# One explicit list of steps for an attention-and-mixing kernel on one core

**The chip, the cores and the metric.** The kernel runs on one core of a Trainium2 chip. The metric is the device time of one execution in microseconds (us). A "span" is the time from the first to the last instruction in a profile; the measured time is 1 to 2 us longer (192.06 against 190.2 in the profiled run of before). Runs are called fast or slow by their time and granted TensorE clock; only fast runs are compared here, and the times and ranges given leave slow ones out.

## The reference, cut to what matters

Four batches, 8 heads, 768 positions, head size 64. Windowed attention with four sink positions makes x; a mixing block follows.

```python
scores = (q @ k.T) / sqrt(64)              # kept: the 4 sinks, and 128 positions back
x      = softmax(scores) @ v               # laid out as (batch, 768, 512)

theta  = x @ w_theta
y      = w_tok_r @ (x * cos(theta)) + w_tok_i @ (x * sin(theta))    # over the 768 positions
u      = x + y
out    = u + max(u @ w_ch, 0)
```

The kernel works on 16 head pairs (four for each batch) and 23 blocks of 128 output rows, plus a last one in halves. Its words, which the argument uses: *scores* (q, k on TensorE, three groups to a pair), *values* (E times v), *theta* (8 matmuls of 512 columns for each of three groups of a batch), *mixing* (12 such matmuls to a block), *channel* (4 to a block). Before scores q and k must be cast to bf16 and transposed; before theta x must be transposed, before channel u.

## The kernel before

The program fixes each engine's order itself: every call puts its instructions at the end of its engines' queues in the order of the source, and semaphores do the rest. It is written as loops over pairs and blocks. This is the loop of the second half:

```python
    for b in range(2, B):
        p = b - 1                                  # batch p is mixed while batch b has its attention
        for hp in range(HP):
            i = b * HP + hp
            blk = (p, hp)
            ...
            scores(i, 0)                           # matmuls AND the exponential that frees their bank
            scores(i, 1)
            ...
            mix(*blk, 0, 8)                        # eight matmuls in one piece
            ...
            scores(i, 2)
            mix(*blk, 8, 12)                       # the other four
            masks(i, 0, 2)
            done(*blk)                             # add(), then dma_u(): the transpose of u
            if hp > 0:
                values(i - 1, 0)
                values(i - 1, 1)
                norm(i - 1)
                dma_x(b, hp - 1)                   # the transpose of one slice of x
            ...
        i = b * HP + HP - 1
        values(i, 0)
        values(i, 1)
        norm(i)
        dma_x(b, HP - 1)                           # the last slice of x ...
        mix(p, 4, 0, 12)
        done(p, 4)
        ...
        theta(b, 0)                                # ... and its first reader
```

Nearly all transposes of u, and those of x from batch 1 on (its last slice excepted), are DMA transposes that SyncE issues, in one queue with all loads and stores:

```python
    def dma_u(b, t):
        nc.sync.dma_start_transpose(out=uT_of(b, t), in_=u_t[b, t].rearrange("p c n -> p (c n)"))

    def done(b, t):
        add(b, t)
        dma_u(b, t)
        waiting.append((b, t))                     # its channel product comes two blocks later
```

The softmax here doesn't subtract the row's maximum and nothing guards it: scores larger than these inputs give would overflow.

## Time and profile before

| | before |
|---|---|
| time, median of 3 runs | 192.33 us (192.32 to 192.81) |
| span of the profiled run | 190.2 us |
| busy: TensorE, VectorE, ScalarE, GpSimd | 169.5, 112.2, 98.2, 73.2 us |
| read from memory | 25.82 MB |
| DMA transposes | 38: 23 of u, 11 of x, 4 of q and k |

The prediction shows the busy shares, the slices, the stretches and the gap at 110 us. One more view belongs beside them. It lists what TensorE's instructions waited for: engine, bank and line of the waiting instruction, the releaser, then us in total, number of waits and the longest.

```profile
PE sc L345 <- DMA xT<-x_nat: 4.0, 2, 2.8
PE sm L345 <- DVE qkT L118: 1.5, 1, 1.5
PE sc L252 <- DMA qkT<-qk: 1.4, 1, 1.4
```

The largest of them are waits of theta (line 345) on a transposed x and on a bank, and of scores (252) on transposed keys.

### The profile page before, as it was taken

To read this page: it belongs to the slowest core of one execution; us is meant where nothing else is said; L and a number is where in the kernel's file an instruction comes from. 1 tells how busy PE (TensorE), PEld (TensorE's weight loads), DVE (VectorE), ACT (ScalarE), POOL (GpSimd) and SP (SyncE) were. 2 spreads that over 40 slices of the span, in tenths; PEclk is the share of its full clock that TensorE was granted. 3 is DMA by queue.
4 is the path that set the end of the run, shared out by engine and by line. 5 is a ranking of instruction groups with operands and counts; after the bars stand their busy time and mean duration, and the time that the engine had idled before them with its cause. 6 is when DMAs were issued, how large, how long until landed. Compare 5 with 4: busy or idle time off the path is not lost.

```text
span 190.2 us, 3823 instructions
## 1 busy us (share of the span) xinstructions
PE 169.5 (89%) x1505; PEld 88.8 (47%) x1505; DVE 112.2 (59%) x193; ACT 98.2 (52%) x129; POOL 73.2 (38%) x95
## 2 busy tenths in 40 slices
PE   7899889599999999698999837999799899999971
PEld 2345465255565565353665413443455444444541
DVE  7556874848656562776777620476757626624442
ACT  3775495977673923699658104497348135300000
POOL 7675556988953737528114610306400000000000
PEclk9999999999999999999999997999999999999997
DMA  5999999999999999999999999379946550514343
GB/s 164 243 332 219 304 394 324 317 337 339 173 357 258 190 295 208 214 306 259 214 156 221 197 177 201 63 133 281 200 96 126 124 127 7 188 30 108 86 138 110
DMA packets 81154, 39.06 MB, mean 205 GB/s; under 512 B 68208, under 2 KB 75632, under 8 KB 81136
## 3 DMA queue, kind: packets, MB, share of 16 engines
q1 hardware_dynamic: 78832, 38.74, 88.6%
q0 software_dynamic: 2304, 0.07, 1.1%
q8 instruction: 12, 0.20, 0.4%
q14 instruction: 6, 0.05, 0.1%
HBM read 25.82 MB, written 6.29 MB: 169 GB/s over the span
## 4 chain that ended last, share of the span: by engine, by line
PE 65%; DMA 12%; DVE 9%; ACT 7%; SPq 3%; issue 2%; POOL 1%; ACTq 0%; POOLq 0%
PE mm L393 21%; PE sc L393 7%; PE mm L421 6%; PE sc L252 6%; PE sc L345 6%; DMA qkT<-qk 5%; PE sm L297 3%; PE sm L225 3%; DMA kf<-in_k_dram 2%; DMA uT<-u 2%; PE sm L378 2%; ACT E L264 2%; DVE x_nat L310 2%; PE sm L443 2%; PE av L297 2%
## 5 line engine op out<-in xcount | busy, mean ns | idle before, releaser
L264 ACT ACTIVATE E<-sc 128x1024 bf16<-128x1024 f32 x48 | 47.3, 1029 | 18.1 <-PE sc L252 12.7
L393 PE MATMUL mm<-zz,wrT 128*128 128x512 bf16 x108 | 41.9, 388 | 0.0
L393 PE MATMUL mm<-zz,wiT 128*128 128x512 bf16 x108 | 41.7, 386 | 0.0
L272 DVE TENSOR_TENSOR E<-E,mask 128x768 bf16<-128x768 bf16 (+1 forms) x28 | 27.3, 974 | 9.2 <-ACT E L264 9.2
L367 DVE TENSOR_TENSOR zz<-cs,x_nat 128x1024 bf16<-128x1024 bf16 x24 | 17.2, 757 | 14.2 <-ACT cs L358 14.1
L421 PE MATMUL mm<-wch,uT 128*128 128x512 bf16 x92 | 23.1, 379 | 0.7 <-DMA uT<-u 0.7
L399 DVE TENSOR_TENSOR u<-mm,x_nat 128x512 bf16<-128x512 f32 x18 | 12.4, 691 | 15.5 <-PE mm L393 15.4
L393 PEld LDWEIGHTS <-wrT 128*128 128x128 bf16 x138 | 13.6, 98 | 16.4 <-issue 2.4
L345 PE MATMUL sc<-wth,xT 128*128 128x512 bf16 x64 | 16.3, 388 | 4.8 <-DMA xT<-x_nat 4.0
L357 ACT ACTIVATE cs<-sc,half_pi 128x1024 bf16<-128x1024 f32 x7 | 7.8, 1117 | 24.6 <-PE sc L345 24.6
L252 PE MATMUL sc<-qkT 64*128 64x256 bf16 x192 | 17.9, 281 | 2.8 <-DMA qkT<-qk 1.4
L393 PEld LDWEIGHTS <-wiT 128*128 128x128 bf16 x138 | 13.7, 99 | 13.8 <-issue 0.8
L297 PEld LDWEIGHTS <-E 128*128 128x128 bf16 x480 | 16.6, 97 | 6.0 <-DVE E L272 1.7
L423 DVE SCALAR_TENSOR_TENSOR of<-mm,u 128x512 f32<-128x512 f32 x23 | 15.8, 689 | 5.1 <-PE mm L421 5.1
L345 PEld LDWEIGHTS <-xT 128*128 128x128 bf16 x96 | 9.2, 99 | 19.9 <-DMA xT<-x_nat 5.3
L114 POOL TENSOR_SCALAR qk<-two 128x768 bf16<-128x768 f32 x8 | 7.5, 951 | 23.5 <-DMA two<-in_k_dram 11.4
L114 POOL TENSOR_SCALAR qk<-qf 128x768 bf16<-128x768 f32 x10 | 10.3, 1028 | 14.1 <-PE sm L225 6.3
L114 POOL TENSOR_SCALAR vx<-vf 128x768 bf16<-128x768 f32 x12 | 12.1, 1011 | 8.5 <-DMA vf<-in_v_dram 7.5
L114 POOL TENSOR_SCALAR qk<-kf 128x768 bf16<-128x768 f32 x10 | 13.6, 1356 | 1.0 <-DMA kf<-in_k_dram 0.6
L252 PEld LDWEIGHTS <-qkT 64*128 64x128 bf16 x192 | 6.9, 96 | 14.6 <-issue 8.8
L421 PEld LDWEIGHTS <-uT 128*128 128x128 bf16 x92 | 8.6, 98 | 10.0 <-DMA uT<-u 1.6
L118 DVE COPY qkT<-sm 128x384 f32<-128x384 f32 (+1 forms) x14 | 7.6, 555 | 7.1 <-PE sm L225 4.1
(103 smaller groups left out, 234.3 us busy)
## 6 DMA issues: line engine op xcount, KB each, us to landing
out_dram<-of SPq DMA_DIRECT2D x23, 256.0 KB, 2.6
vf<-in_v_dram SPq DMA_DIRECT2D x12, 384.0 KB, 7.3
qf<-in_q_dram SPq DMA_DIRECT2D x10, 384.0 KB, 5.8
kf<-in_k_dram SPq DMA_DIRECT2D x10, 384.0 KB, 6.5
wf<-in_moe_w_tok_r_dram SPq DMA_DIRECT2D x6, 384.0 KB, 7.2
wf<-in_moe_w_tok_i_dram SPq DMA_DIRECT2D x6, 384.0 KB, 5.9
two<-in_q_dram SPq DMA_DIRECT2D x2, 768.0 KB, 7.6
two<-in_k_dram SPq DMA_DIRECT2D x2, 768.0 KB, 5.9
```

What stands on the lines that cost most here:

```text
L114: nc.gpsimd.tensor_scalar(out=out, in0=in_, scalar1=1.0, scalar2=1.0, op0=ALU.mult, op1=ALU.mult)
L252: nc.tensor.matmul(sc[:, e, 256 * part:256 * part + n], lhsT=kT[r, m * P:(m + 1) * P], rhs=qT[r, m * P:m * P + n], start=not biased, stop= ...
L264: nc.scalar.activation(out=E[:, :, 512 * c:512 * (c + 1)], in_=sc, func=AF.Exp, scale=SCALE)
L272: nc.vector.tensor_tensor(out=E[:, :, r], in0=E[:, :, r], in1=m2, op=ALU.mult)
L297: nc.tensor.matmul(avp[:, t, :], lhsT=lhsT, rhs=rhs, start=(j == 0), stop=(j == len(seq) - 1), skip_group_check=True)
L345: nc.tensor.matmul(thp[st], lhsT=xT_t[b][:, cb, 2 * g + st, :], rhs=wth[:, cb, :], start=(cb == 0), stop=(cb == NC - 1), skip_group_check= ...
L357: nc.scalar.activation(out=cs[:, :, 0, :], in_=thp, func=AF.Sin, bias=half_pi)
L367: nc.vector.tensor_tensor(out=z_t[b][:, 2 * g + st, :, :].rearrange("p o (c n) -> p o c n", c=HP), in0=cs[:, st, :, :].rearrange("p o (c n ...
L393: nc.tensor.matmul(y_t[b, t][:, cols], lhsT=wT[i][:, t, sc, :], rhs=z_t[b][:, sc, i, cols], start=(j == 0), stop=(j == 2 * NT - 1), skip_g ...
L399: nc.vector.tensor_tensor(out=u_t[b, t][:, cbs, :], in0=y_t[b, t].rearrange("p (c n) -> p c n", c=HP)[:, cbs, :], in1=x_t[b][:, cbs, t, :] ...
L421: nc.tensor.matmul(wp[:, cols], lhsT=uT[:, cb, :], rhs=wch[:, cb, cols], start=(cb == 0), stop=(cb == NC - 1), skip_group_check=parts > 1)
L423: nc.vector.scalar_tensor_tensor(out=of[:, cols], in0=wp[:, cols], scalar=0.0, in1=u[:, cols], op0=ALU.max, op1=ALU.add)
```

## The change

The intent: TensorE is the bound, so give it at every moment something that is ready. The loops are replaced by about 850 steps that name each action, its arguments and, behind the @, its engine or PSUM bank. What was one call becomes two or more: a transpose and its eviction, a scores group and its exponential, a mixing block in six pieces of two matmuls.

```diff
-    for hp in range(HP):
-        i = HP + hp
-        ...
-        scores(i, 2)
-        mix(0, t, 0, 12)
-        masks(i, 0, 2)
-        done(0, t)
     ... (all loops of the schedule go)
+    def mix(how, b, t, sc):
+        for i in range(2):
+            nc.tensor.matmul(bank(how, "py", b, t), lhsT=wT[i][:, t, sc, :], rhs=new("z", b)[:, sc, i, :],
+                             start=(sc == i == 0), stop=(sc == NT - 1 and i == 1), skip_group_check=True)
+    def turn_u(how, b, t):
+        tp = as16(bank(how, "pu", b, t), NC)
+        for cb in range(NC):
+            nc.tensor.transpose(out=tp[:, cb, :], in_=new("u", b, t)[:, cb, :], identity=ident)
+    ...
+    PLAN = """
+    ...
+    mx.0.1.0@mm l.w.3.0 p.0.1.1 t.k.6@sm mx.0.2.0@mm p.0.1.0 c.q.7@p l.v.4 mx.0.1.1 e.k.6@d mx.0.2.1 c.q.5@p
+    t.q.6@sm mx.0.2.2 c.w.3.0@p c.w.3.1@p x.4.1 mx.0.2.3 t.k.7@sm s.4.0@sc c.v.4@p s.4.2@sc e.q.6@d x.4.0
+    ...
+    """
+    for step in PLAN.split():
+        step, _, how = step.partition("@")
+        name, *args = step.split(".")
+        STEPS[name](how, *(int(a) if a.isdigit() else a for a in args))
```

To read a step: `mx.0.1.2` is piece 2 of the mixing of batch 0, block 1; `l`, `c`, `t`, `e` load, cast, transpose and evict (`c.q.7@p`: queries of pair 7 cast on GpSimd; `a` is ScalarE, `d` VectorE); `s` and `x` are scores and exponential, `v` and `n` values and norm, `th`, `cs`, `p` theta, sine, product; `tu`+`eu` transpose u on TensorE and evict it, `du` does it by DMA (so too `tx`+`ex`, `dx`; `dq` for q and k); `ch`, `o`, `so` channel, its result, its store; `warm` is a matmul on zeros. The steps' order in the list is again the order in each engine's queue. Buffers change a little: ten staging buffers in place of eleven and four double ones, five cast buffers for two, seven value buffers for four.

## The prediction

> **What bounds the kernel now.** I read the page's busy shares first, then each engine's share in 40 slices:
>
> ```profile
> PE 169.5 (89%) x1505; PEld 88.8 (47%) x1505; DVE 112.2 (59%) x193; ACT 98.2 (52%) x129; POOL 73.2 (38%) x95
> ...
> PE   7899889599999999698999837999799899999971
> ...
> PEclk9999999999999999999999997999999999999997
> DMA  5999999999999999999999999379946550514343
> ```
>
> TensorE is the only engine near full, but 89% is not work. The timeline gives the real price of each matmul as the distance between neighbouring starts: 512-wide ones start 0.216 us apart although each lasts 0.38. I priced every group of the by-shape list this way:
>
> - 512-wide: mixing 276, channel 92, theta 96, together 464 x 0.216 = 100.2
> - 256-wide of the last block: 32 x 0.108 = 3.5
> - value products: 32 heads x 0.47 = 15.0
> - scores: 16 pairs x 0.99 = 15.8; their 12 bias matmuls 2.4
> - transposes: 60 in fp32 x 0.11 = 6.6; 130 in bf16 x 0.055 = 7.2
> - 7 warm-up matmuls 1.5
>
> The sum is 152 us. The span is 190.2, so about 38 us are lost. The busy time by stretch says where:
>
> ```profile
> core 0: us, PE busy (x) PEld busy (x) DVE busy (x) ACT busy (x) POOL busy (x), PEclk, DMA share, GB/s
> 0.00:17.00 17.00, 14.62 (x88) 6.35 (x88) 10.59 (x24) 10.26 (x12) 12.45 (x27) 1.00 0.95 241
> 17.00:40.00 23.00, 19.30 (x245) 11.28 (x244) 16.40 (x33) 16.24 (x23) 14.53 (x22) 1.00 1.11 324
> 40.00:110.00 70.00, 66.20 (x692) 38.06 (x691) 45.16 (x78) 44.10 (x63) 38.57 (x40) 1.00 1.17 245
> 110.00:120.00 10.00, 5.99 (x20) 2.12 (x19) 2.15 (x4) 2.03 (x2) 0.82 (x1) 0.83 1.09 194
> ```
>
> Going through the whole TensorE timeline and subtracting each group's price from the distance to the next group, I get these losses: 0 to 40 us about 17 (1.25 before the first matmul included), 40 to 110 about 8, 110 to 120 about 6, 120 to 187 about 6, and 3 to 4 from the last matmul to the end. With slightly lower prices in that pass they add to 40, which is the same thing. The timeline shows the third one plainly:
>
> ```profile
> 110.27 0.59 PE L345 MATMUL sc<-wth,xT 128*128 128x512 bf16 x2
> 113.65 0.39 PE L345 MATMUL sc<-wth,xT 128*128 128x512 bf16 x1 [2.79 <-DMA xT<-x_nat]
> 115.27 1.47 PE L345 MATMUL sc<-wth,xT 128*128 128x512 bf16 x5 [1.23 <-DMA xT<-x_nat]
> 116.53 0.63 PE L393 MATMUL mm<-zz,wrT 128*128 128x512 bf16 x1
> 116.96 0.63 PE L393 MATMUL mm<-zz,wiT 128*128 128x512 bf16 x1
> ```
>
> Theta of batch 2 waits for activations that the DMA transposes; the first six matmuls of the mixing after it start 0.43 apart instead of 0.216. The waits of the SyncE queue say why that transpose is late: it and the loads stand in one queue behind transposes that wait for a VectorE result.
>
> ```profile
> SPq L409 <- DVE u L399: 16.1, 4, 7.4
> SPq L409 <- DVE of L423: 8.6, 5, 2.4
> ```
>
> **What the Trainium skill says.** Perfetto Trace Analysis, Identifying the Most-Contended Engine, says that matmul busy time is no measure of distance to the roofline because matmuls are pipelined; the trace agrees (169.5 busy, 152 by starts). TensorE: Matmul & The Clock Gate, Part 1, says that an idle TensorE falls back to half clock after a window of about 3.4 us, with 512-wide starts 426.7 ns apart cold and 215.7 warm. The trace agrees at 116.5 (0.43 against 0.216), and the first 16 us look cold too (the bias matmuls at 14.25 take 0.43 each), though the granted-clock row does not show it there. Part 4 says that transposes do not count as busy for that gate in the same way; the opening is mostly transposes and stays slow for 16 us, which fits but doesn't prove it. Perfetto Trace Analysis, Optimization Strategy, advises interleaving stages that load different engines. That is what the new list does.
>
> **The change, part by part.** I counted the steps of the list and compared the instruction order of both programs.
>
> *Added on TensorE.* Nine of the 23 DMA transposes of u become four TensorE transposes each (36), four of the 11 of x become six each (24): 60 x 0.055 = 3.3 us. Warm-up matmuls go from 7 to 16: 9 x 0.216 = 1.9. All else has the same count. Need: 152 + 5 = 157 us.
>
> *Added elsewhere.* Thirteen evictions at about 0.4 to 0.56 us, 6 us on ScalarE and VectorE together; the norms of batch 3 head by head, 8 x 0.75 instead of 4 x 1.19, +1.2 on VectorE; some casts from GpSimd to ScalarE and VectorE. *Removed:* sines of four theta groups in two 1.07 halves instead of four of 0.64, -1.7 on ScalarE. Adding all steps at the durations of before gives about 107 us ScalarE, 124 VectorE, 65 GpSimd: still below TensorE, and all of it beside TensorE.
>
> *Moved.* (a) The first DMA transpose now comes after all of batch 0 and half of batch 1's mixing; until then the SyncE queue holds only loads and a few stores, so it can't be held by a late u. (b) Theta of batch 2 gets the last slice of x from TensorE, with mixing pieces and scores of batch 1 between the norms and theta. (c) The queries and keys of pairs 12 to 14 are transposed one stage earlier; of pair 15 some 30 matmuls (over 6 us) before their use, where before landed in 4.3. (d) Scores of batch 3 lie between the mixing of batch 2 instead of before it, so the exponentials have cover. (e) Every tile asks for one of two "mm", two "sm" banks or two pairs; no bank is set aside for the late norms.
>
> What remains of each loss:
>
> - 0 to 40 us, 17: the first load lands about 4 us in, GpSimd needs 15 us and ScalarE 16 for the steps up to the scores of pair 3 against TensorE's 16, and by theta of batch 0 some 8 MB must be in, 30 us at about 270 GB/s. Little slack is left for any order. I keep 10.
> - 40 to 110, 8: largely waits for an eviction with nothing to put before it. Pieces of two matmuls fill them: 4.
> - 110 to 120, 6: gone, 0.5 kept.
> - 120 to 187, 6: the wait for transposed keys near 136 goes, the chain of the last block stays: 2.
> - After the last matmul, 3.5: unchanged, a last result and a store.
>
> Sum: 157 + 10 + 4 + 0.5 + 2 + 3.5 = 177 us of span. The measured time stood 2.1 above the span (192.33 to 190.2): 179. The dense list gives every TensorE instruction its successor, and whoever chose 850 steps one by one will have pruned harder than my halves; I shade it to 178.
>
> **Rivals.**
>
> *The opening binds and gets worse.* For: all four engines and the DMA need nearly the same time up to 40 us of TensorE work (ScalarE 40, VectorE 37, GpSimd 36, 15 MB of loads), so one late item shifts everything; the list loads all of the token weights before batch 0 is mixed. Against: before moved 324 GB/s in the stretch from 17 to 40, and without transposes beside it the same rate should hold longer. Would give 184 to 190.
>
> *Fixed order meets real durations.* A list tuned on estimated durations stalls TensorE wherever an eviction is later than assumed, since a wrong guess in a strict order blocks all behind it; with two banks of each kind shared by seven kinds of tile, small waits of 0.2 to 0.5 us could come at each of some 80 bank turns. Half of them would be 15 us and leave 186 to 190. Against: before lives with just as many turns and loses only 8 us in 70.
>
> *All gaps close.* TensorE as the pure bound: 157 + 6 opening + 3.5 + 2.1 = 169. For: the list plainly spends warm-up matmuls on the cold clock. Against: nothing in the trace lets the loads land sooner.
>
> **Range and chances.** The main case gives 178, the two bad rivals 184 to 190, the good one 169; 170 to 187 holds most of it. For 188.5 or more, nearly the whole gain has to be eaten: 0.09 together. A time above 196 would need a stage that has no cover at all, which I see nowhere: 0.02.
>
> **What would show it.** Right: no TensorE wait over 1 us on transposed x or keys after 60 us; no stretch at half clock after 20 us; TensorE loss from 40 us to the last matmul below 8 us; theta of batch 1 (82 us before) ending by about 77; DMA transposes 38 down to 25. Wrong: TensorE waits on VectorE or ScalarE that add to over 12 us, or the end of theta of batch 0 later than the 36.7 us of before, meaning that the opening lost.

## The result

| | before | after |
|---|---|---|
| time, median of 4 fast runs | 192.55 us (192.32 to 192.81) | 175.48 us (175.09 to 176.17) |
| span of the profiled run | 190.2 | 174.5 |
| TensorE, VectorE, ScalarE, GpSimd busy | 169.5, 112.2, 98.2, 73.2 | 163.0, 120.3, 102.0, 66.0 |
| read from memory | 25.82 MB | 25.82 MB |
| DMA transposes, of u, x, q and k | 23, 11, 4 | 14, 7, 4 |
| median from issue to landing of those | 3.4, 3.1, 4.3 us | 2.5, 2.8, 3.9 us |

The ratio is 0.9117, with a 95% interval of 0.9084 to 0.9151. Ratios are here the mean time of one kernel's fast runs over that of the other's of the same rounds, so not quite the ratio of the medians quoted. The change is faster by 9%, and 2.5 us faster than predicted.

The page of after, with the busy shares and the 40 slices of the span:

```profile
PE 163.0 (93%) x1549; PEld 90.8 (52%) x1574; DVE 120.3 (69%) x220; ACT 102.0 (58%) x129; POOL 66.0 (38%) x84
...
PE   7668899999999999999999999999999999999991
...
PEclk9999999999999999999999999999999999999998
```

From the sixth slice (22 us) to the last but one there is no digit but 9 in TensorE's row, where before falls below it all along, once to 3; and the granted clock has no dip. TensorE's busy time fell although it has more to do. Part of that is real: a matmul at half clock is recorded longer. Part is not: the page counts 1549 matmuls and 1574 weight loads, where before has 1505 of both. The 25 missing matmuls are records that the trace lost: 14 of mixing, 4 of theta, 5 of channel, 2 of the bias. At 0.216 us each they would be 5.4 us. A stretch in which nothing is recorded is not always idle; the weight loads give it away.

By stretch (us from the start; busy time and count for TensorE, its weight loads, VectorE, ScalarE and GpSimd; clock; DMA share; GB/s):

```profile
0.00:17.00 17.00, 12.37 (x103) 5.38 (x103) 10.78 (x31) 9.64 (x13) 9.73 (x20) 1.00 0.87 233
17.00:40.00 23.00, 21.69 (x284) 13.66 (x281) 19.52 (x37) 19.31 (x24) 16.70 (x24) 1.00 1.08 338
40.00:110.00 70.00, 68.85 (x780) 41.22 (x787) 53.15 (x92) 51.85 (x72) 35.85 (x38) 1.00 0.97 225
110.00:120.00 10.00, 9.95 (x60) 4.78 (x60) 7.01 (x13) 8.48 (x10) 2.04 (x2) 1.00 1.05 211
```

The counts say more than the busy times: from 17 to 40 us TensorE now gets through 284 matmuls, where before did 245; from 40 to 110, 780 and more (787 weight loads) for 692; in the bad stretch from 110 to 120, 60 for 20. The DMA share in the third row fell from 1.17 to 0.97, and the GB/s from 245 to 225.

Theta of batch 2, the place of the gap before, as TensorE's timeline shows it (start, duration, engine, line, output and inputs, count):

```profile
109.60 1.89 PE L321 MATMUL sc<-wth,xT 128*128 128x512 bf16 x8
111.33 0.38 PE L347 MATMUL sm<-z,wrT 128*128 128x512 bf16 x1
111.54 0.38 PE L347 MATMUL sm<-z,wiT 128*128 128x512 bf16 x1
111.76 1.89 PE L321 MATMUL sc<-wth,xT 128*128 128x512 bf16 x8
```

Eight theta matmuls, two of mixing, eight theta: no line has a wait in brackets, and the starts within are 0.216 us apart. The view of waits for after:

```profile
PE sm L226 <- POOL qk L109: 1.4, 1, 1.4
PE sm L226 <- DVE qk L113: 1.4, 1, 1.4
PE sm L162 <- DVE zeros L126: 1.2, 1, 1.2
PE mm L226 <- POOL qk L109: 0.9, 2, 0.7
```

All four belong to the opening: the transposes of the first q and k (line 226) wait for casts, and the first warm-up for its zeros. After 18 us the recorded waits of TensorE add to about 1.2 us. On SyncE's queue the wait of the u transposes on VectorE's sum, 16.1 us before, is down to:

```profile
SPq L364 <- DVE u L351: 9.4, 2, 6.7
```

It is two waits instead of four, and nothing on TensorE waits behind it. (Before's four all lie after 115 us, so they are not what made the transpose at the gap late; more on this below.)

### The profile page after: what moved, and what is told of

Read it like the earlier page. It is cut to its first block, busy times and chain, and to the rows that moved or that the text cites. A ratio compares the mean times of both kernels' runs of the same rounds, so it can differ in the third digit from the quotient of the medians.

```text
span 174.5 us, 3910 instructions
## 1 busy us (share of the span) xinstructions
PE 163.0 (93%) x1549; PEld 90.8 (52%) x1574; DVE 120.3 (69%) x220; ACT 102.0 (58%) x129; POOL 66.0 (38%) x84
## 3 DMA queue, kind: packets, MB, share of 16 engines
HBM read 25.82 MB, written 6.29 MB: 184 GB/s over the span
## 4 chain that ended last, share of the span: by engine, by line
PE 72%; DMA 16%; POOL 5%; SPq 2%; issue 2%; ACT 1%; DVE 0%; POOLq 0%
PE mm L347 16%; PE sm L347 15%; PE sc L321 9%; DMA wf<-in_moe_w_tok_i_dram 8%; PE mm L368 6%; PE sm L368 5%; PE sm L292 5%; PE sc L255 5%; DMA qf<-in_q_dram 4%; DMA vf<-in_v_dram 3%; POOL raw L109 2%; SPq L190 2%; PE mm L226 2%; POOL qk L109 2%; PE mm L388 2%
## 5 line engine op out<-in xcount | busy, mean ns | idle before, releaser
L276 DVE TENSOR_TENSOR E<-E,mask 128x2048 bf16<-128x2048 bf16 (+1 forms) x28 | 28.7, 1047 | 0.5 <-ACT E L269 0.4
L347 PE MATMUL mm<-z,wiT 128*128 128x512 bf16 x73 | 27.7, 379 | 0.5 <-issue 0.3
L347 PE MATMUL mm<-z,wrT 128*128 128x512 bf16 x73 | 27.7, 380 | 0.2
L347 PE MATMUL sm<-z,wrT 128*128 128x512 bf16 x59 | 22.4, 379 | 0.2
L347 PE MATMUL sm<-z,wiT 128*128 128x512 bf16 x57 | 21.6, 379 | 0.1
L330 DVE TENSOR_TENSOR z<-cs,x 128x1024 bf16<-128x1024 bf16 x24 | 18.2, 787 | 2.8 <-ACT cs L325 2.8
L109 POOL TENSOR_SCALAR qk<-kf 128x768 bf16<-128x768 f32 (+1 forms) x13 | 14.4, 1109 | 12.9 <-DMA kf<-in_k_dram 12.8
L109 POOL TENSOR_SCALAR qk<-qf 128x768 bf16<-128x768 f32 (+1 forms) x12 | 13.4, 1121 | 7.7 <-DMA qf<-in_q_dram 4.4
L325 ACT ACTIVATE cs<-sc 128x1024 bf16<-128x1024 f32 x12 | 12.3, 1023 | 4.3 <-PE sc L321 3.3
L301 DVE TENSOR_TENSOR x<-sm,rec 128x384 bf16<-128x384 f32 x23 | 12.8, 558 | 0.8
```

The lines of the kernel that those rows point to most:

```text
L109: nc.gpsimd.tensor_scalar(out=out, in0=in_, scalar1=1.0, scalar2=1.0, op0=ALU.mult, op1=ALU.mult)
L276: nc.vector.tensor_tensor(out=E[:, :, lo:lo + n], in0=E[:, :, lo:lo + n], in1=m2, op=ALU.mult)
L301: nc.vector.tensor_tensor(out=new("x", b)[:, hp, :, D * e:D * (e + 1)], in0=avp[:, :, 0:D], in1=rec.to_broadcast([P, NT, D]), op=ALU.mult)
L325: nc.scalar.activation(out=new("cs", b, g)[:, :, n, :], in_=pair("pt", b, g), func=AF.Sin, **({} if n else {"bias": half_pi}))
L330: nc.vector.tensor_tensor(out=new("z", b)[:, 2 * g + st, :, :].rearrange("p o (c n) -> p o c n", c=HP), in0=new("cs", b, g)[:, st, :, :].r ...
L347: nc.tensor.matmul(bank(how, "py", b, t), lhsT=wT[i][:, t, sc, :], rhs=new("z", b)[:, sc, i, :], start=(sc == i == 0), stop=(sc == NT - 1 ...
```

## The experiments

Twelve kernels ran, in four sets; each set has its own runs of before on the same chip, and every kernel gave the right result. Edits are given in the notation of the steps. "After's place" means the ratio of after, 0.9117, or 0.9125 (0.9087 to 0.9163) when it was run again in the second set as a control:

> The changed kernel once more, unaltered, so that the three others of this job are compared on the same chip: 175.5 us plus or minus 0.8.

It took 175.82 us. Two runs of the same program are thus 0.3 us apart in their medians; differences of a microsecond mean little.

### Fine pieces: the mixing block in one piece again

```diff
-mx.0.1.0@mm l.w.3.0 p.0.1.1 t.k.6@sm mx.0.2.0@mm p.0.1.0 ... mx.0.1.1 ... mx.0.1.4 t.q.7@sm c.k.5@p mx.0.1.5
+            l.w.3.0 p.0.1.1 t.k.6@sm             p.0.1.0 ...          t.q.7@sm c.k.5@p mx.0.1.0@mm mx.0.1.1 ... mx.0.1.5
 (all 23 blocks; each stands where its last piece stood)
```

> The changed list with the six pieces of each mixing product put together where the last piece stood; same steps, same engines, same bank choices. Theory A (pieces of two matmuls between the waits are a large part of the gain): 4 to 8 us slower, 179.5 to 183.5, the TensorE idle time spread over many waits of 0.3 to 1 us on ScalarE and VectorE. Rival B (the coarse order with theta, scores and channel steps has enough cover): below 177.5.

It took 191.69 us (191.09 to 193.39), ratio 1.0003 (0.9929 to 1.0077). The whole gain is gone, some 16 us, where I had expected half of that at most (4 to 8 us). The same work, the same engines and the same transposes, so where does it go? First, after near 42 us:

```profile
41.93 0.49 PE L226 MATMUL sm<-ident,qk 128*128 128x128 f32 x3
42.26 0.38 PE L347 MATMUL mm<-z,wrT 128*128 128x512 bf16 x1
42.47 0.38 PE L347 MATMUL mm<-z,wiT 128*128 128x512 bf16 x1
42.78 0.61 PE L255 MATMUL sc<-qkT 64*128 64x256 bf16 x8
43.33 0.39 PE L347 MATMUL mm<-z,wrT 128*128 128x512 bf16 x1
```

And the kernel with whole blocks in the same region:

```profile
40.59 0.34 PE L255 MATMUL sc<-qkT 64*128 64x256 bf16 x4 [0.74 <-ACT E L269]
40.86 0.30 PE L263 MATMUL sc<-qkT 64*32 64x128 bf16 x8
42.70 0.90 PE L226 MATMUL sm<-ident,qk 128*128 128x128 f32 x3 [1.54 <-POOL qk L109]
43.39 0.63 PE L347 MATMUL mm<-z,wrT 128*128 128x512 bf16 x1
43.82 0.63 PE L347 MATMUL mm<-z,wiT 128*128 128x512 bf16 x1
```

Transposes and scores now stand side by side. Each is short, and each waits for another engine: for a bank that ScalarE must clear with an exponential, for a cast of GpSimd. In after a pair of mixing matmuls, 0.43 us, lies between two of them, and takes the place of the wait. Here the waits come bare, and behind them the clock is at half: the mixing from 43.39 on starts 0.43 us apart, though no single wait before it was longer than 1.54 us. Going through this kernel's whole timeline with one price for each kind of matmul, I get losses of 10.8 us between 30 and 60 us, where after loses 3.0 in the same pass. That is about half of the 17.2 us by which the two spans differ; by a second pass the rest is lost after 60 us, in many short stretches. Half clock is a small part of it: the ten matmuls from 43.39 to 47.65 pay 2.1 us.

That has a rival: perhaps the blocks are merely late, since each stands at its last piece.

```diff
-mx.0.3.0@mm l.ch.0 e.k.5@d mx.0.3.1 c.k.8@p l.ch.2 mx.0.3.2 mx.0.3.3 ... mx.0.3.4 ... mx.0.3.5
+mx.0.3.0@mm mx.0.3.1 mx.0.3.2 mx.0.3.3 mx.0.3.4 mx.0.3.5 l.ch.0 e.k.5@d c.k.8@p l.ch.2 ...
 (all 23 blocks; each stands as early as its inputs allow)
```

> The changed list with each mixing product whole, but as early as its data are there in the list (after the batch's last product with x and the eviction of its weights) instead of where its last piece stood. It tells apart two readings of the first run with whole products (191.7 us): if late placement was the harm, 176 to 180 us; if it is that 12 matmuls in one block cannot fill the waits of scores, theta and transposes, 183 us or more, with waits on ScalarE and VectorE in 35 to 60 and 80 to 115 us as there.

It took 191.08 us (191.04 to 191.73 in three fast runs; a slow one took 194.82), ratio 0.9928 (0.9848 to 1.0007). Early or late, the gain is gone, so the late place was not the harm. The waits have only changed their names. The longest sums are now:

```profile
PE sc L255 <- ACT E L269: 3.1, 7, 0.5
PE sm L347 <- DVE z L330: 2.9, 2, 1.8
```

Seven waits of at most half a microsecond for a bank are what two matmuls of mixing (0.43 us) could have covered. What these two runs do not show is that fine pieces alone, put into before, would bring 16 us: both lists were made for fine pieces and only then coarsened, and other edits to the finished list, below, cost 5 to 11 us without touching the pieces.

### x on TensorE: one part of the change, put into before

```diff
-                dma_x(b, hp - 1)
+                if (b, hp) == (2, 3):
+                    turn_x(b, hp - 1, "act")
+                else:
+                    dma_x(b, hp - 1)
 ...
-        dma_x(b, HP - 1)
+        if b == 3:
+            dma_x(b, HP - 1)
         mix(p, 4, 0, 12)
+        if b == 2:
+            turn_x(b, HP - 1, "act")
```

> The kernel before with one part of the change: the last two slices of x of batch 2 are transposed by TensorE and evicted by ScalarE instead of by DMA. Theory A (the 6 us lost at 110 to 120 come from these two late transposes and the half clock that follows the idle time): 186.5 to 188.5, TensorE waits on transposed x gone and starts of 0.216 us right after. Rival B (the wait is taken over by the next one, transposed keys of batch 3 or sines): 190.5 or more, with the loss moved to 120 to 140.

It took 186.40 us (185.52 to 187.21), ratio 0.9736 (0.9669 to 0.9802), where the fast runs of before in this set have a median of 191.69: two slices of x, twelve transposes on TensorE, bring some 5 us in before. (That it is faster is clear; whether by 2% is not.) The gap that the prediction shows has closed:

```profile
111.86 1.89 PE L345 MATMUL sc<-wth,xT 128*128 128x512 bf16 x8
113.59 0.38 PE L393 MATMUL mm<-zz,wrT 128*128 128x512 bf16 x1
```

Theta runs through, and the mixing behind it is at full clock. This is the prediction's term "110 to 120", in size (5.5 us) and in that late transposes of x and the half clock behind them make it up. Why they were late is another matter. SyncE's queue in before:

```profile
104.10 0.87 SPq L142 DMA_DIRECT2D two<-in_q_dram  x1
105.07 4.99 SPq L409 DMA_TRANSPOSE uT<-u  x1
110.16 1.24 SPq L329 DMA_TRANSPOSE xT<-x_nat  x1
112.11 1.25 SPq L329 DMA_TRANSPOSE xT<-x_nat  x1
```

The first of the two slices of x was ready at 105.6 us and the second at 108.1, by VectorE's timeline, but they stood behind a transpose of u. That u was itself ready at 104.2. It didn't wait; its issue took 4.99 us, just behind a load of 768 KB, where the ones after it took 1.2. The gain does not simply add to the effect above: the two together would be more than the whole 17 us, so the parts share idle time.

### u on TensorE: back to the DMA

```diff
-tu.0.3@sm ... eu.0.3@a        (nine blocks; nine evictions go too)
+du.0.3
```

> The changed list with all nine TensorE transposes of u put back to DMA transposes at the same place, their evictions taken out; TensorE need falls by 2.0 us. Theory A (TensorE transposes are what keeps the SyncE queue free for loads in the first 80 us): the queue stands behind late u again, loads come late, and the time rises by 3 us or more, to 178.5 or above, with TensorE waits on DMA of w or q, k. Rival B (the order of the TensorE work alone covers it): 173 to 175.5, TensorE waits on transposed u below 1 us in all.

It took 180.65 us (179.77 to 181.58; a slow run took 183.63), ratio 0.9434 (0.9374 to 0.9494): 5 to 6 us slower than after. The size came, but not in the way that I had in mind. I thought that SyncE's queue would be held up by transposes waiting for u, and that loads would come late. The trace shows the reverse. TensorE's timeline:

```profile
72.34 1.89 PE L368 MATMUL mm<-wch,uT 128*128 128x512 bf16 x4 [3.72 <-DMA uT<-u]
```

and SyncE's queue for the u that this line waits for:

```profile
64.87 2.01 SPq L190 DMA_DIRECT2D qf<-in_q_dram  x1
66.93 1.88 SPq L364 DMA_TRANSPOSE uT<-u  x1
```

The u had long been ready (VectorE added no u between 57.1 and 75.5 us). Its transpose stands behind loads, the last of which took 2.01 us to issue, where the one before it took 0.43; the queue's wait just before that load took 0.02 us, so neither a late u nor a missing buffer held it. The transpose then landed at 72.30, 5.4 us after its issue, where the median of after's u is 2.5, and the channel product waits for it. What makes issue and landing long between the loads was not tested. TensorE has no other wait over 1 us after the opening, so no load came late for it. After the gap the next mixing matmuls start 0.42 us apart, at half clock.

### q and k of pairs 8 to 11: to the DMA as well

```diff
-    LONG = set(range(3 * HP))
+    LONG = set(range(2 * HP))
-t.k.9@mm ... e.k.9@d          (q and k of four pairs: 24 transposes, 8 evictions)
+dq.9
```

> The changed list with the queries and keys of pairs 8 to 11 transposed by DMA (issued right after their casts) in place of 24 fp32 TensorE transposes and 8 evictions: TensorE need falls by 2.6 us. Theory A (past 20 us the kernel is bound by TensorE work itself, so work taken out comes off the time): 2 to 2.8 us faster than the changed kernel of this job, 172.7 to 173.5. Rival B (the queue of SyncE is held behind these transposes and later loads or transposes of u arrive late, as in the run with all u by DMA): no faster, or slower by up to 4 us, with TensorE waits on DMA between 70 and 100 us.

It took 186.68 us (185.84 to 186.83; a slow run took 188.64), ratio 0.9672 (0.9631 to 0.9712), 11 us slower than after. TensorE's two longest waits and the queue's line that answers to the first:

```profile
PE sc L255 <- DMA qkT<-qk: 7.2, 1, 7.2
PE sm L292 <- POOL vx L109: 3.2, 1, 3.2
```

```profile
73.58 7.85 SPq L236 DMA_TRANSPOSE qkT<-qk  x3
```

The scores could have begun at 73.6 us, where TensorE runs out of other work, and begin at 80.8. In just that time the queue issues the three transposes of pairs 8 to 10. The queries of pair 8 were cast from 70.6 to 71.9 us; a store and a load stand ahead, the first transpose is issued at 73.58 and lands at 80.79, 7.2 us later, where the median of after's four is 3.9. So most of this wait is the landing of the transpose and not its place in the queue. The second wait, at 103.7 us, is for a value tile whose cast stood in GpSimd's queue behind that of queries for which GpSimd had waited 9.4 us on their load: here a load did come late, as the second theory had it. The saving on TensorE, 24 transposes in fp32 at 0.11 or 2.6 us, is lost four times over. (The loads of these pairs also take another layout in this kernel, which the kernel's DMA transpose expects; its share is not told apart.)

### Four transposes that have time

```diff
-tu.1.1@sm ... eu.1.1@a        (likewise u of batch 1, blocks 2 and 0; tx.2.0+ex.2.0)
+du.1.1                        (each later in the list, at a place where the queue is free)
```

> The changed kernel with four TensorE transposes that the list gives more than 8 us before their use put back to DMA, at places of the SyncE queue where nothing behind is due: u of blocks 1, 2 and 0 of batch 1 and the first slice of x of batch 2. TensorE need falls by 3 x 0.22 + 0.33 = 1.0 us, four evictions go. Theory A (past the opening the kernel is bound by TensorE's own work, and a DMA transpose with time enough costs nothing): 0.7 to 1.0 us faster, ratio 0.906 to 0.909. Rival B (any transpose in that queue delays the loads and transposed keys behind it): slower, ratio 0.914 or more, with TensorE waits on DMA between 90 and 120 us.

It took 174.85 us (173.87 to 175.92), ratio 0.9070 (0.9021 to 0.9120). The size is what was expected, about 1 us, but the interval overlaps that of after, so alone it shows only that nothing is lost.

### Engines by a rule

```diff
-c.k.1.0@d e.k.1.0@d c.q.1.1@a ew.1.1@d ...      (48 steps: 18 casts, 30 evictions)
+c.k.1.0@p e.k.1.0@a c.q.1.1@p ew.1.1@a ...      (every cast on GpSimd, every such eviction on ScalarE)
```

> The changed list in its order, but with the engine of each step by a plain rule in place of its own choice: every cast on GpSimd (18 more there), every eviction of a transpose on ScalarE (30 more there). Theory A (order is what counts, engines have room: ScalarE 102 us and GpSimd 66 us of 174): slower by less than 2 us. Rival B (in the first 45 us all engines are within a few us of TensorE's need, so a rule overfills ScalarE and GpSimd there): slower by 4 us or more, lost before 50 us, with TensorE waits on GpSimd casts and ScalarE evictions.

It took 184.92 us (184.00 to 186.30), ratio 0.9594 (0.9547 to 0.9642): 9 us slower than after. No engine is full (ScalarE stays well below TensorE), and the largest single wait comes early:

```profile
PE mm L226 <- POOL qk L109: 3.8, 1, 3.8
```

GpSimd's own timeline at that time:

```profile
6.60 2.48 POOL L158 DMA_DIRECT2D vsink<-in_v_dram  x4
10.07 0.51 POOL L109 TENSOR_SCALAR qk<-qf 128x384 bf16<-128x384 f32 x1
```

The issue of the sink loads takes GpSimd 2.5 us, and the cast that in after goes to VectorE (`c.q.0.0@d`) now stands behind it and two more casts. Further waits in the opening, 2.1 us of them for ScalarE's evictions, and a stretch at half clock follow. The end of theta of batch 0, at 34.6 us in after, is at 41.3 here, that of batch 1, near 73, near 81, and the span is 8.8 us longer: nothing is made good later, as one would expect of a list that leaves TensorE hardly any idle time in which to catch up.

### Warm-up matmuls

```diff
-warm.7@sm ... warm.4@mm       (fewer_warm: the nine scattered ones; no_warm: all sixteen)
```

> The changed list without the nine warm-up matmuls that are scattered through the opening; the seven at the start stay. Theory A (the opening is bound by loads and casts, the warm-ups only fill holes): 175.5 us plus or minus 0.6, TensorE need down 1.9 us, loss in the first 20 us up by as much. Rival B (they keep the clock up, which is what made the opening quicker): the opening runs at 0.43 us per 512-wide start until about 17 us as in the kernel before, and the time rises by 2 to 4 us, to 177.5 to 179.5.

> The changed list without any of its 16 warm-up matmuls. Theory A (the opening waits for loads and casts, so the clock there is worth little; the run with seven of them showed half clock until about 16 us and a span of 173.9): within 0.8 us of the changed kernel of this job. Rival B (clock in the opening decides): slower by 2 us or more, with the end of theta of batch 0 later by as much.

Without nine: 176.34 us (175.60 to 176.64), ratio 0.9208 (0.9162 to 0.9254). Without any: 175.41 us (174.84 to 176.15), ratio 0.9098 (0.9061 to 0.9134), beside after's 175.82 in the same set. The first ratio looks like a small loss, and its time is just above what theory A allowed, but its set had restless runs of before (189.75 to 192.53 in the fast ones), its time is within 0.9 us of after's, and its profiled span, 173.9, is no longer than after's 174.5. The second removes all and loses nothing. In the profile of fewer_warm TensorE stays at half clock until about 16 us, in that of after it is at full clock from 6.5; but in that of after_again, the same program, only from about 13, and in that of no_warm, which has no warm-ups, from about 13 too. In the first 18 us TensorE waits for loads and casts in any case. The profiles rather hint that the warm-ups cost a little: theta of batch 0 ends at 32.8 and 32.9 us in the two kernels without any (no_warm and lean_list), and at 34.3 to 34.6 in four profiles with all sixteen (after, after_again, two_queues, four_by_dma).

### The opening: a second queue for four loads

```diff
+        eng = nc.scalar if name == "q" and s is not None else nc.sync
-                nc.sync.dma_start(out=f.rearrange(...), in_=src.rearrange(...))
+                eng.dma_start(out=f.rearrange(...), in_=src.rearrange(...))
```

> The changed kernel with the four half loads of q of the first two pairs issued from ScalarE's queue instead of SyncE's; all else equal. SyncE takes about 0.5 us to issue each of the first loads, one after the other, and issues the load of q of pair 2, which lands at 12.4 us, only at 4.87. Theory A (the opening is bound by how soon the loads are issued and land): 1 to 2 us faster, ratio to the kernel before 0.903 to 0.907, the first casts and scores earlier by as much. Rival B (the engines' own work in the opening, casts on GpSimd above all, binds): within 0.5 us of the changed kernel, ratio 0.910 to 0.914.

It took 176.09 us (175.01 to 176.91), ratio 0.9128 (0.9081 to 0.9174): after's place. The first whole q was issued at 4.04 us instead of 4.87, and the opening was no shorter (theta of batch 0 ended at 34.5 us). The issue of these four loads is not what bounds it.

### A leaner list

```diff
-warm.15@sm ... warm.4@mm                             (all sixteen)
-tu.0.0@sm eu.0.0@a  tu.0.5@sm eu.0.5@d               (and the four of the experiment above)
+du.0.0              du.0.5                           (at free places in the queue)
```

> What the other runs point to, in one list: no warm-up matmuls, and six TensorE transposes that have over 8 us until their use put back to DMA (u of blocks 0 and 5 of batch 0, of blocks 0, 1 and 2 of batch 1, the first slice of x of batch 2). TensorE need past the opening falls by 5 x 0.22 + 0.33 = 1.4 us, six evictions go. If TensorE's own work binds past the opening and the queue has room at these places: 1.2 to 1.8 us faster than the changed kernel, 173.5 to 174.5 us, ratio to the kernel before 0.901 to 0.906. If the two added transposes delay the loads of queries behind them: ratio 0.910 or more, with TensorE waits on GpSimd casts or on DMA between 70 and 95 us.

It took 173.46 us (173.04 to 175.52; a slow run took 176.33), ratio 0.9045 (0.8992 to 0.9099), the lowest of all kernels tried. The intervals of it and of after overlap slightly, so "faster than after by some 0.8%" is likely rather than shown. The longest wait that is left stands in the opening:

```profile
PE sm L226 <- POOL qk L109: 4.5, 2, 4.1
```

### What could not be tried

Two lists in which the PSUM banks follow a rule (in turn, or one kind of tile to each kind of bank) were built, and both deadlock: with two banks of a kind, a tile can wait for a bank that is only freed by a step standing behind it. What the choice of banks is worth in time stays open. So does the worth of the changed buffer counts, which no run tests on its own.

## Why the prediction was right, and where it was off

**TensorE as the bound, the losses as the prize.** Right. The list adds 5 us of TensorE work and takes 16 us off the span.

**The sum.** Here are the terms as predicted and as the same pass over after's timeline gives them, the lost records put back at their price:

| term | predicted | after |
|---|---|---|
| TensorE work | 157 | 154.4 |
| lost from 0 to 40 us | 10 | 11.5 |
| 40 to 110 | 4 | 3.5 |
| 110 to 120 | 0.5 | 0.1 |
| 120 to the last matmul | 2 | 0.8 |
| after it | 3.5 | 3.9 |
| span | 177 | 174.2 (profile: 174.5) |

The five losses sum to 19.8 us, where 20 were predicted. (The split hangs on the prices: a second pass with somewhat lower ones gives losses of 42.8 us before and 22.7 after, with 6.0 from 40 to 110. The difference of 20 us stands; a single term is good to some 2 us.) Of the sum, the term that was mis-sized is the first. The step "with slightly lower prices in that pass they add to 40, which is the same thing" is the one that failed: the work had been priced at 152, the losses in a pass in which the same work costs 149.4, so the two sum to 192 where the span is 190.2. Carried over to after, work at the high price and losses at the low one counted some 2.6 us twice. With one set of prices the prediction would have said 174 to 175 of span. The step from span to time was 0.4 too long as well: it set the median of other runs against the span of the profiled one, and in that run itself the difference was 1.9 us before (1.7 after).

**0 to 40 us, 10 kept.** Lost 11.5 us, so a little worse than thought, though better than before's 17; theta of batch 0 ends near 34.6 us instead of 36.7. The first rival, an opening that gets worse, did not come. Neither the clock (no_warm) nor the issue of the first loads of q (two_queues) bounds the opening. The waits and the chain name loads and GpSimd's casts, but no run has settled which load or cast it is; this stays open. The 1.9 us for nine more warm-ups were counted as a cost. The medians show none beyond the noise (175.41 us without any, 175.82 with all), the profiles one of at most 1.8 us for all sixteen (theta of batch 0 over at 32.8 in place of 34.3 to 34.6).

**40 to 110, "pieces of two matmuls fill them".** The step held, and the new order leans on it more than the 4 us that it was given: whole_mix and whole_mix_early lose all 16, in this stretch and after it. It was given only what before lost in that stretch. But in the new order the pieces probably also cover what the new order itself brings up: more transposes, evictions and bank turns than before had. This reading is argued from the two runs, and no run isolates it.

**110 to 120, "gone".** Right, and shown alone by before_x_on_pe, some 5 us.

**120 to the end, 2 kept.** Lost 0.8. The wait for transposed keys is gone, as predicted; no run tested that part, (c), on its own, nor the cover for the exponentials, (d).

**(a), the queue "can't be held by a late u".** The effect was real, 5 us in u_by_dma, but the reason given for it was wrong where it could be checked. The prediction laid the late x at 110 us to a queue standing behind transposes that wait for VectorE, and showed 16.1 us of such waits in four. All four lie after 115 us in before's trace, the longest from 115.8 to 123.3, behind the gap. At the gap a u that was ready took 4.99 us to issue, and in u_by_dma a ready u stood behind slow loads and took 5.4 us to land. In both the data were in time and the transpose was late in issue or landing, with loads around it. That the loads make it so is the likely reading and not a tested one. (Between 85 and 99 us before's queue does show three transposes of u that start 1.5 to 3.6 us after the instruction ahead of them, so late results can have had a part; no run separates it.)

**(e), the banks.** Open, as said above.

**The other engines.** Predicted 107, 124 and 65 us for ScalarE, VectorE and GpSimd; 102.0, 120.3 and 66.0 came, all below TensorE. engines_by_kind shows that this sum is not the point: in the list an engine that is half idle costs 9 us when one of its steps comes at the wrong time.

**"Fixed order meets real durations".** This rival expected small waits at every turn of a bank, and after has almost none after 18 us. It is still right about the danger: every list that was disturbed without being made anew (u_by_dma, qk_by_dma, engines_by_kind, whole_mix) gave back a third to all of the gain.

**The signs named in advance.** No TensorE wait over 1 us on transposed x or keys after 60 us, no half clock after 20 us, 4.4 us lost between 40 us and the last matmul (7.4 in the second pass; below 8 was named), theta of batch 1 over near 73 us (by 77), 25 DMA transposes: all came.

## What to carry to other kernels

Where one engine is the bound and its gaps are short waits for others, cut its long independent work into pieces about as long as those waits and put one behind every step that something must follow; here the finished list lost its whole gain when twelve matmuls stood in place of two. A transpose belongs on the DMA if its reader is far off and the queue is free of loads at that place (here some landed after 2.5 us and others, among loads, after 5.4 and 7.2), and on TensorE otherwise. Before a total of waits is taken as the cause of a gap, look up when these waits were. Price the work and measure the losses with the same numbers, and compare matmul counts with weight-load counts before reading a gap as idle time.

## What the Trainium skill lacked or had wrong

- TensorE: Matmul & The Clock Gate, Part 1, gives the rise of the clock as about 4 us into sustained matmul activity, give or take 500 ns. That is no figure for an opening that is broken by waits (the page itself calls the point run-variable): two profiles of one and the same program rose at 6.5 and at about 13 us, and one with nine warm-ups fewer at about 16, with spans of 174.5, 174.8 and 173.9. Warming up was worth nothing here (175.41 us without, 175.82 with). The window of about 3.4 us of idle time, which the prediction quotes from there, is not the length of one gap: in whole_mix the clock was at half at 43.39 us after waits of at most 1.54. The page's distances of 426.7 and 215.7 ns agree with the trace (0.43 and 0.216 us).
- DMA: Bandwidth & Descriptors, Issuing engines are not separate DMA queues, says that a second issuing engine saves only the sequencer's time of issue; two_queues agrees (176.09 us). That section lacks the other side: on one issuing engine a transpose whose data are ready stands behind whatever is slow to issue, 4.99 us in before, and among loads it is long in landing, 5.4 us in u_by_dma and 7.2 in qk_by_dma, where after's medians are 2.5 and 3.9.
- None of the pages that I read says how fine to interleave. Here, in a list made for pieces of two, these gave 175.5 to 175.8 us and blocks of twelve 191.1 to 191.7.
- Perfetto Trace Analysis does not tell its reader to check whether matmul records are missing: 25 of 1574 are in after, seen only against the count of weight loads.
